# Turning k, q and u of the last two batches by transposing DMA, and a ring of three in the planned order of row loads

## The chip, the core and the metric

The kernel runs on one core of a Trainium2 chip. The metric is the device time of one execution in microseconds, as the median of several runs. One further execution was recorded by the hardware profiler; every duration of a single instruction below is from that execution.

## What is computed

Four batches, eight heads, 768 tokens, head size 64. A retention recurrence gives y, which is laid side by side over the heads as x of 768 tokens by 512 channels; a mixer follows, first over the tokens, then over the channels:

```python
for t in range(S):
    state = gamma * state + einsum('bhd,bhe->bhde', k[:, :, t], v[:, :, t])
    y[:, :, t] = scale * einsum('bhd,bhde->bhe', q[:, :, t], state)
x = y.transpose(0, 2, 1, 3).reshape(B, S, H * D)
h = relu(x.T @ w_tok1) @ w_tok2          # over the 768 tokens, 256 hidden
u = x + h.T
out = u + relu(u @ w_ch1) @ w_ch2        # over the 512 channels, 1536 hidden
```

## The kernel before

The recurrence is done in blocks of 128 tokens. For each batch b there are four **fronts** (b, p), one for each pair of heads (p, 128 channels together), and one **back**.

A front loads the f32 rows of k, q and v of two heads (`kf`, `qf`, `vf`, 384 KB each, L227 to L245), and casts them to f16 tiles `k16` (VectorE, L257), `q16` and `v16` (GpSimd, L264), each of 128 tokens by six blocks by 128 channels. `turn` (L271 to L288) then makes the transposed tiles `kT` and `qT`, channels on partitions: six transposes of 128x128 on TensorE into a PSUM tile `fa` (L277), and one copy out of PSUM (L286), on ScalarE but for the first batch's kT. The state products (L299), the masked products within a block (L338, which read kT and qT), y (L359 and L362), the two token matmuls (L413 and L433) and the addition of the result to x (VectorE, L440) follow. The sum, u, is cast to f16 by GpSimd in two halves (tile `u16`, L447), turned by six more transposes (L457) and copied to `uT` (ScalarE, L466).

A back takes uT of all four fronts of its batch. Twice (once for each half of the tokens) it runs 48 matmuls against `wc1` (L497) with a Relu behind every four (L510), and then three groups of twelve matmuls against `wc2` (L526), each followed by the addition of x (L535) and a store of 256 KB (L542).

The order of all this is not that of the code: `arrange` is a list scheduler with estimated durations. It gives out the next operation by start time and priority; a front's work on TensorE goes ahead of a back's, so a back fills the time in which a front waits. What it gives out is then emitted, and each engine runs its own rows strictly in that order. For the row loads and stores the queue is SP's: a DMA at the head that waits for data holds every DMA behind it. A load is told apart only by an estimated transfer time, `dma`, which is added to a single clock called `free["DMA"]`; nothing limits in the plan how many DMAs SP has given out and not yet moved.

Two more details. In the first two batches q is loaded with longer runs (L232), which interleaves its tokens, and the copy to qT undoes that. And 54 matmuls of a zero tile (L184) fill TensorE in the first batch while it waits for data.

Of the kernel before, what the change touches and what calls it, by code (L numbers as in the profile page):

```python
# [11 lines left out]
F16 = mybir.dt.float16  # L12
# [5 lines left out]
def kernel(  # L18
# [11 lines left out]
    nc = tc.nc  # L30
    B, H, S, D = q.shape
    P = 128
    NC = S // P
    HC = NC // 2
    NP = H // 2
# [10 lines left out]
    sb = ctx.enter_context(tc.tile_pool(name="sb", bufs=1))  # L46
# [31 lines left out]
    for p in range(NP):  # L78
# [5 lines left out]
        out=mask, in_=mask, compare_op=ALU.is_ge, fill=0.0,  # L84
# [4 lines left out]
    for t in r16:  # L89
# [6 lines left out]
    wc2 = const_p.tile([P, NF, C], F16, name="wc2")  # L96


    BUFS = dict(kf=4, qf=4, vf=4, k16=3, q16=3, v16=4, kT=4, qT=4, U=3, am=8, x16=2, h1=4, u16=3,
                x=3, uT=3, h2=2, o=3, r16=NR, fa=5, ba=3)  # L100
    SEM, GUARD = 80, 100
    EARLY, LATE, DIRECT = 1000, 12, 3
    ops = []

    class Slot:
# [15 lines left out]
    def arrange():  # L121


        way = {}
        for op in reversed(ops):
            if op.first is not None:
                way[op] = way.get(op, 0) + op.lat + SEM
                for d in op.deps:
                    way[d] = max(way.get(d, 0), way[op])
        for op in ops:  # L130
            if op.first is not None:
                op.prio = (op.prio[0], 0, EARLY * op.first - way[op], op.first)
        free = dict(PE=5000, ACT=5000, DVE=4600, POOL=4000, SP=1300, DMA=1300)
        taken = {t: [] for t in BUFS}
        todo, order = list(ops), []
        while todo:
            best = []
            for op in todo:
                if any(d.end is None for d in op.deps):
                    continue  # L140
                start = free[op.eng]
                for d in op.deps:
                    if d.eng == op.eng and (d.dma or d.eng == "PE"):
                        continue
                    start = max(start, d.end + (30 if d.eng == op.eng else SEM) + op.guard)
                more = {}
                for s in op.takes:
                    q = taken[s.tag]
                    n = len(q) + more.get(s.tag, 0) - BUFS[s.tag]
                    more[s.tag] = more.get(s.tag, 0) + 1  # L150
                    if n >= 0:
                        old = q[n]
                        if any(u.end is None for u in old.users):
                            break
                        start = max([start] + [u.end + SEM for u in old.users])
                else:
                    best.append((start, op))
            t = min(b[0] for b in best)

            eng = min(best, key=lambda b: (b[0], b[1].prio))[1].eng  # L160
            start, op = min((b for b in best if b[1].eng == eng and b[0] <= t + 20),
                            key=lambda b: b[1].prio)
            free[op.eng] = start + op.occ
            op.start = start
            if op.dma:
                free["DMA"] = max(free["DMA"], start + 50) + op.dma
                op.end = free["DMA"] + 1600
            else:
                op.end = start + op.lat
            for s in op.takes:  # L170
                taken[s.tag].append(s)
            todo.remove(op)
            order.append(op)
        return order
# [3 lines left out]
    def tile_of(slot, pool, shape, dtype, tag=None):  # L178
        tag = tag or slot.tag
        slot.tile = pool.tile(shape, dtype, name=tag, bufs=BUFS[tag])  # L180
        if pool is ps:

            for _ in range(idle[0]):
                nc.tensor.matmul(slot.tile, zero[:, :P], zero, start=True, stop=True)  # L184
            idle[0] = 0
        return slot.tile
# [11 lines left out]
    x_add, uT_done, y_done, t1_done, t2_done = {}, {}, {}, {}, {}  # L198
# [3 lines left out]
    def front(b, p):  # L202
        first = b == 0
# [3 lines left out]
        def op(eng, occ, lat, emit, deps=(), takes=(), uses=()):  # L207
            n[0] += 1
            pr = (0 if eng == "PE" else 1, b, n[0] + LATE * p, p)
            o = Op(eng, pr, occ, lat, emit, deps, takes, uses, guard=g if eng == "PE" else 0)  # L210
            o.first = p if first else None
            return o
# [3 lines left out]
        X, UT = xs[b], uTs[b]  # L216
        pc = slice(p * P, (p + 1) * P)

        def half(hf):
            return slice(hf * HC, (hf + 1) * HC)  # L220


        sl, ld = {}, {}
        for nm, src in (("k", k), ("q", q), ("v", v)):
            sl[nm] = Slot(nm + "f")

            def emit(nm=nm, src=src):  # L227
                t = tile_of(sl[nm], sb, [P, 2 * NC, D], FP)
                rows = src[b, 2 * p:2 * p + 2]
                if nm == "q" and b < 2:  # L230

                    dma = nc.sync.dma_start(  # L232
                        out=t.rearrange("p (h f i) d -> p h f (i d)", h=2, f=2),
                        in_=rows.rearrange("h (f p i) d -> p h f (i d)", f=2, p=P))
                else:
                    dma = nc.sync.dma_start(out=t, in_=rows.rearrange("h (c p) d -> p (h c) d", p=P))  # L236
                if b == 1:
                    tc.add_manual_dep(
                        dma.ins, wops["c1", 1].ins.ins.name,
                        mybir.DependencyInfo(mybir.DependencyClass.Sync, mybir.DependencyReason.DATA),  # L240
                        reason="the weights come first")
            ld[nm] = Op("SP", (0, b, p), 100, 100, emit,
                        deps=[load_done[-1]] + ([wops["c1", 1]] if b == 1 else []),
                        takes=[sl[nm]], dma=1200 if nm == "q" and b < 2 else 1750)
            load_done.append(ld[nm])  # L245

        K, Q, V = Slot("k16"), Slot("q16"), Slot("v16")
# [23 lines left out]
        def turn(src, dst, dep, eng):  # L271
            T = Slot("fa")

            def emit():
                T.tile = tp = tile_of(T, ps, [P, 512], FP).bitcast(F16)
                for c in range(NC):
                    nc.tensor.transpose(tp[:, c * P:(c + 1) * P],  # L277
                                        src.tile[:, c].rearrange("p h d -> p (h d)"), ident16)
            t = op("PE", 340, 500, emit, [dep, t1_done.get(b * NP - 1) if b > 1 else None], [T], [src])

            def emit():
                d, o = tile_of(dst, sb, [P, S], F16), T.tile[:, :S]
                if dst is QT and b < 2:
                    d = d.rearrange("d (f p i) -> d f i p", f=2, i=HC)
                    o = o.rearrange("d (f i p) -> d f i p", f=2, i=HC)
                (nc.scalar.copy if eng == "ACT" else nc.vector.tensor_copy)(d, o)  # L286
            occ = dict(ACT=1350 if dst is QT and b < 2 else 700, DVE=470)[eng]
            return op(eng, occ, occ + 90, emit, [t], [dst], [T])  # L288
        kt = turn(K, KT, kc, "DVE" if first else "ACT")
        qt = turn(Q, QT, qc, "ACT")  # L290


        ST, US, RS = Slot("fa"), Slot("U"), Slot("r16")
# [126 lines left out]
            h1 = tile_of(H1, sb, [P, NJ, P], F16)  # L420
            nc.scalar.activation(h1.rearrange("p j c -> p (j c)"), T1.tile[:, :NJ * P], AF.Relu)
        hr = op("ACT", 300, 380, emit, [t1], [H1], [T1])
        tt = []
        T = Slot(FA)
        for hf in range(2):
            T2, U16 = Slot(FA), Slot("u16")

            def emit(hf=hf, T2=T2):
                acc = tile_of(T2, ps, [P, 512], FP)
# [13 lines left out]
            x_add[b, p, hf] = ad  # L443

            def emit(hf=hf, U16=U16):
                u = tile_of(U16, sb, [P, HC, P], F16)
                nc.gpsimd.tensor_copy(u, X.tile[:, half(hf), pc])  # L447
            uc = op("POOL", 450, 510, emit, [ad], [U16], [X])
            if first:
                T = Slot(FA)  # L450

# [9 lines left out]
            if first or hf == 1:  # L461
                def emit(hf=hf, T=T):
                    if UT.tile is None:
                        tile_of(UT, sb, [P, NP, S], F16)
                    t = slice(hf * SH if first else 0, (hf + 1) * SH)
                    nc.scalar.copy(UT.tile[:, p, t], T.tile[:, t])  # L466
                tk = [UT] if (b, "uT") not in uT_done else []
                dep = [] if tk else [uT_done[b, "uT"]]
                e = op("ACT", 380 if first else 700, 480 if first else 800, emit, [tt[-1]] + dep, tk,
                       [T] if tk else [T, UT])  # L470
                if tk:
                    uT_done[b, "uT"] = e
                for s in range(2):
                    if not first or s == hf:
                        uT_done[b, p, s] = e
        return kc, qc, vc


# [123 lines left out]
```

## Time and profile before

| | |
|---|---|
| median of three runs | 217.54 us (216.63 to 217.7) |
| the profiled execution | 216.79 us, of which the span of its instructions is 215.1 us |
| VectorE, ScalarE, GpSimd busy | 113.2, 113.3 and 61.4 us |
| DMA | 29.42 MB, of it 25.17 MB on the hardware queue that SP feeds |
| granted TensorE clock | 0.999 |

The times of runs are of the whole execution; the profile's times count from the span's start, and the 1.7 us between span and execution lie around it. TensorE's matmuls are pipelined: the duration of a row of matmuls holds the fill and drain, so the cost of a group is better read from the start of the next row. What the engines wait for is shown with the prediction.

### The profile page before, as it was taken

How to read it: one execution, taken by the hardware profiler on the slowest of the kernel's cores; microseconds unless marked ns; L12 is line 12 of the kernel's file. 1: busy time of each engine (PE TensorE's matmuls, PEld its weight loads, DVE VectorE, ACT ScalarE, POOL GpSimd, SP SyncE). 2: the span in 40 equal slices, each digit the busy share in tenths (PEclk: the TensorE clock that was granted, in tenths of full speed). 3: DMA queues.
4: the chain of work that ended last, by engine and by line, in shares of the span. 5: the costliest groups of instructions: out<-in, count | busy, mean ns of one | idle time of the engine just before them, and what ended most of it. 6: DMA issues, size and time to landing. Idle time of an engine off the chain costs nothing.

```text
span 215.1 us, 5027 instructions
## 1 busy us (share of the span) xinstructions
PE 206.7 (96%) x2042; PEld 129.6 (60%) x2042; DVE 113.2 (53%) x291; ACT 113.3 (53%) x229; POOL 61.4 (29%) x107
## 2 busy tenths in 40 slices
PE   6898898999999999999999999999999999999993
PEld 1564486664667677676667676667645645545552
DVE  6387895017998876886865886673112012012021
ACT  6246467772887537668536787344721712703700
POOL 2337943023345455453444113302100000000000
PEclk9999999999999999999999999999999999999999
DMA  6999999999999999999921100012002012012012
GB/s 171 245 242 233 191 203 208 222 216 265 222 235 237 253 240 217 217 223 259 217 105 49 52 2 3 0 67 83 0 10 111 28 46 103 0 49 98 0 52 98
DMA packets 73591, 29.42 MB, mean 137 GB/s; under 512 B 62688, under 2 KB 70112, under 8 KB 73568
## 3 DMA queue, kind: packets, MB, share of 16 engines
q1 hardware_dynamic: 69904, 25.17, 53.8%
q0 software_dynamic: 3664, 3.93, 11.2%
q8 instruction: 16, 0.26, 0.5%
q14 instruction: 7, 0.06, 0.1%
HBM read 26.74 MB, written 6.29 MB: 154 GB/s over the span
## 4 chain that ended last, share of the span: by engine, by line
PE 85%; SPq 5%; DMA 4%; ACT 2%; DVE 1%; issue 1%; POOL 0%; DVEq 0%
PE ba L497 30%; PE ba L526 29%; PE fa L277 4%; PE fa L433 4%; PE fa L413 4%; DMA kf<-in_k_dram 4%; PE fa L338 3%; SPq L236 3%; PE fa L362 3%; SPq L232 2%; PE fa L457 2%; PE fa L359 2%; PE fa L299 2%; PE ba L413 1%; PE ba L184 1%; ACT qT L286 1%
## 5 line engine op out<-in xcount | busy, mean ns | idle before, releaser
L526 PE MATMUL ba<-wc,h 128*128 128x512 f16 (+1 forms) x300 | 68.1, 371 | 0.0
L497 PE MATMUL ba<-uT,wc 128*128 128x384 f16 x384 | 68.1, 326 | 0.0
L510 ACT ACTIVATE h<-ba 128x384 f16<-128x384 f32 x96 | 46.6, 491 | 40.0 <-PE ba L497 39.5
L497 PEld LDWEIGHTS <-wc 128*128 128x128 f16 x384 | 35.9, 98 | 22.5
L535 DVE TENSOR_TENSOR o<-x,ba 128x512 f32<-128x512 f32 (+1 forms) x25 | 16.6, 664 | 59.2 <-PE ba L526 59.0
L526 PEld LDWEIGHTS <-h 128*128 128x128 f16 x300 | 27.7, 98 | 26.2
L345 DVE TENSOR_TENSOR am<-fa,mask 128x384 f16<-128x384 f32 x64 | 33.0, 550 | 7.8 <-PE fa L338 7.5
L264 POOL CAST q<-qf 128x768 f16<-128x768 f32 x16 | 13.4, 840 | 32.4 <-DMA qf<-in_q_dram 23.2
L390 POOL CAST x<-x 128x384 f16<-128x384 f32 x30 | 15.1, 512 | 23.8 <-ACT x L373 14.8
L286 ACT COPY qT<-fa 128x768 f16<-128x768 f16 x16 | 18.1, 1129 | 6.8 <-PE fa L277 6.8
L447 POOL CAST u<-x 128x384 f16<-128x384 f32 x32 | 15.9, 507 | 19.4 <-DVE x L440 17.5
L257 DVE TENSOR_SCALAR k<-kf,gk 128x384 f16<-128x384 f32 x32 | 13.8, 472 | 9.0 <-DMA kf<-in_k_dram 9.0
L184 PE MATMUL fa<-zero 128*128 128x512 f16 x54 | 15.8, 424 | 2.4 <-DVE zero L52 1.3
L311 DVE SCALAR_TENSOR_TENSOR U<-U,gp,fa 128x64 f32<-128x64 f32 x64 | 17.6, 275 | 1.0
L373 ACT ACTIVATE x<-fa,gy 128x192 f32<-128x192 f32 (+1 forms) x42 | 15.1, 419 | 5.0 <-PE fa L362 4.5
L264 POOL CAST v<-vf 128x768 f16<-128x768 f32 x16 | 13.2, 828 | 12.1 <-PE fa L362 7.3
L466 ACT COPY uT<-fa 128x768 f16<-128x768 f16 x12 | 9.5, 794 | 13.2 <-PE fa L457 13.2
L318 ACT ACTIVATE r<-U 64x320 f16<-64x320 f32 x16 | 7.5, 466 | 13.6 <-DVE U L311 13.4
L440 DVE TENSOR_TENSOR x<-x,fa 128x384 f32<-128x384 f32 x24 | 12.6, 548 | 3.7 <-PE fa L433 3.6
L362 PE MATMUL fa<-v,am 128*128 128x64 f16 x192 | 14.1, 193 | 0.0
L413 PEld LDWEIGHTS <-wt 128*128 128x128 f16 x192 | 11.8, 98 | 2.6 <-issue 0.4
L433 PEld LDWEIGHTS <-wt 128*128 128x128 f16 x192 | 11.6, 98 | 2.0
(52 smaller groups left out, 195.0 us busy)
## 6 DMA issues: line engine op xcount, KB each, us to landing
kf<-in_k_dram SPq DMA_DIRECT2D x16, 384.0 KB, 6.5
qf<-in_q_dram SPq DMA_DIRECT2D x16, 384.0 KB, 6.3
vf<-in_v_dram SPq DMA_DIRECT2D x16, 384.0 KB, 6.1
out_dram<-o SPq DMA_DIRECT2D x23, 256.0 KB, 2.0
wc<-in_moe_w_ch_dram POOLq DMA_DIRECT2D x1, 1536.0 KB, 19.1
wc<-in_moe_w_ch_dram POOLq DMA_DIRECT2D x1, 1024.0 KB, 11.8
wt<-in_moe_w_tok_dram POOLq DMA_DIRECT2D x2, 384.0 KB, 7.0
wc<-in_moe_w_ch_dram POOLq DMA_DIRECT2D x1, 512.0 KB, 6.9
```

Source lines behind the costliest of these rows:

```text
L184: nc.tensor.matmul(slot.tile, zero[:, :P], zero, start=True, stop=True)
L264: nc.gpsimd.tensor_copy(t.rearrange("p c h d -> p h c d"), src.tile.rearrange("p (h c) d -> p h c d", h=2))
L286: (nc.scalar.copy if eng == "ACT" else nc.vector.tensor_copy)(d, o)
L311: nc.vector.scalar_tensor_tensor(U[:, c], U[:, c - 1], gp[:, p:p + 1], o, ALU.mult, ALU.add)
L345: nc.vector.tensor_tensor(am, src[:, :HC], mask, ALU.mult)
L362: nc.tensor.matmul(o[:, j * D:(j + 1) * D], AM[2 * hf + j].tile[:, i], V.tile[:, c, j], start=(c == 0), stop=(c == 0 or j == 1))
L413: nc.tensor.matmul(acc[:, jt * P:(jt + 1) * P], wt1[:, i, jt * P:(jt + 1) * P], X16.tile[:, i], start=(i == 0), stop=(i == NC - 1))
L433: nc.tensor.matmul(acc[:, i * P:(i + 1) * P], wt2[:, jt, t], H1.tile[:, jt], start=(jt == 0), stop=(jt == NJ - 1))
L497: nc.tensor.matmul(acc[:, :SH], w[:, ct, f * P:(f + 1) * P], UT.tile[:, ct, sh * SH:(sh + 1) * SH], start=(ct == 0), stop=(ct == NP - 1))
L510: nc.scalar.activation(H2.tile[:, ft], A.tile[:, :SH], AF.Relu)
L526: nc.tensor.matmul(A.tile[:, :CW], H2.tile[:, ft, i * P:(i + 1) * P], wc2[:, ft, cs], start=(ft == 0), stop=(ft == NF - 1))
L535: nc.vector.tensor_tensor(o[:, :CW], X.tile[:, sh * HC + i, cs], A.tile[:, :CW], ALU.add)
```

## The change

Three things are changed, all in `arrange` and `front`.

1. For the batches from the third on (`XK = XQ = XU = 2`), `turn` is replaced for k and q by `crossbar`: one transposing DMA on SP's queue, from `k16` or `q16` straight to `kT` or `qT` (192 KB each, both in SBUF). No PSUM tile, no TensorE work and no ScalarE copy is left of it. The gate that held the turns of the later batches until the last first token matmul of the batch before (`t1_done`) is not among the crossbar's conditions.
2. For the same batches u is cast by GpSimd into one tile `u16w` for both halves (two buffers), and one transposing DMA on SP's queue makes that front's part of `uT`. 24 transposing DMAs are added in all: eight each for k, q and u.
3. The planner gets a list `ring` of the planned ends of SP's transfers. A DMA on SP isn't planned to start before the third last one given out has been moved (`RING = 3`). This moves loads and stores against each other in SP's queue from the second batch on.

`LONG = 2` only gives the old condition `b < 2` a name.

```diff
-    BUFS = dict(... u16=3,
+    BUFS = dict(... u16=3, u16w=2,
+    LONG, XK, XQ, XU, XBAR, RING = 2, 2, 2, 2, 1500, 3
...
-        todo, order = list(ops), []
+        todo, order, ring = list(ops), [], []
...
                 start = free[op.eng]
+                if op.dma and op.eng == "SP" and len(ring) >= RING:
+                    start = max(start, ring[-RING])
...
                 op.end = free["DMA"] + 1600
+                if op.eng == "SP":
+                    ring.append(free["DMA"])
...
-        kt = turn(K, KT, kc, "DVE" if first else "ACT")
-        qt = turn(Q, QT, qc, "ACT")
+
+        def crossbar(src, dst, dep):
+            def emit():
+                d = tile_of(dst, sb, [P, S], F16)
+                return nc.sync.dma_start_transpose(
+                    out=d.rearrange("d (c t) -> d c t", t=P),
+                    in_=src.tile.rearrange("p c h d -> p (c h d)"))
+            return Op("SP", (-1, b, p), 100, 100, emit, [dep], [dst], [src], dma=XBAR)
+        kt = crossbar(K, KT, kc) if b >= XK else turn(K, KT, kc, "DVE" if first else "ACT")
+        qt = crossbar(Q, QT, qc) if b >= XQ else turn(Q, QT, qc, "ACT")
...
-        tt = []
-        T = Slot(FA)
+        tt, uc = [], None
+        wide = b >= XU
+        T, UW = Slot(FA), Slot("u16w")
...
-            T2, U16 = Slot(FA), Slot("u16")
+            T2, U16 = Slot(FA), UW if wide else Slot("u16")
...
-                u = tile_of(U16, sb, [P, HC, P], F16)
+                if wide:
+                    u = tile_of(U16, sb, [P, NC, P], F16) if hf == 0 else U16.tile
+                    u = u[:, half(hf)]
+                else:
+                    u = tile_of(U16, sb, [P, HC, P], F16)
                 nc.gpsimd.tensor_copy(u, X.tile[:, half(hf), pc])
-            uc = op("POOL", 450, 510, emit, [ad], [U16], [X])
+            new = hf == 0 or not wide
+            uc = op("POOL", 450, 510, emit, [ad, uc] if wide else [ad], [U16] if new else [], [X] if new else [X, U16])
+            if wide:
+                continue
...
+        if wide:
+            def emit():
+                if UT.tile is None:
+                    tile_of(UT, sb, [P, NP, S], F16)
+                return nc.sync.dma_start_transpose(
+                    out=UT.tile[:, p].rearrange("d (c t) -> d c t", t=P),
+                    in_=UW.tile.rearrange("p c d -> p (c d)"))
+            tk = [UT] if (b, "uT") not in uT_done else []
+            e = Op("SP", (-1, b, p), 100, 100, emit, [uc] + ([] if tk else [uT_done[b, "uT"]]), tk,
+                   [UW] if tk else [UW, UT], dma=XBAR)
+            if tk:
+                uT_done[b, "uT"] = e
+            for s in range(2):
+                uT_done[b, p, s] = e
```

What this does to the engines' own orders is seen at three places. The first is SP's queue at the start of the third batch. Before, the loads of its first two fronts (k, q, v) stand there with one store of the first back between them:

```order
L236 DMA kf<-in_k_dram 128x12x64
L236 DMA qf<-in_q_dram 128x12x64
L236 DMA vf<-in_v_dram 128x12x64
L542 DMA out_dram<-o 128x512
L236 DMA kf<-in_k_dram 128x12x64
L236 DMA qf<-in_q_dram 128x12x64
L236 DMA vf<-in_v_dram 128x12x64
```

Now the same queue, from the same load on (the code's lines have moved: L236 is L241, the transposing DMAs of k and q are L298):

```order
L241 DMA kf<-in_k_dram 128x12x64
L241 DMA qf<-in_q_dram 128x12x64
L241 DMA vf<-in_v_dram 128x12x64
L241 DMA kf<-in_k_dram 128x12x64
L241 DMA qf<-in_q_dram 128x12x64
L298 DMA_TRANSPOSE kT<-k_1285 128x6x128
L298 DMA_TRANSPOSE qT<-q_1330 128x6x128
L241 DMA vf<-in_v_dram 128x12x64
L298 DMA_TRANSPOSE kT<-k_1407 128x6x128
L298 DMA_TRANSPOSE qT<-q_1447 128x6x128
L241 DMA kf<-in_k_dram 128x12x64
```

Three stores of the first back now stand ahead of these rows, among the loads of the second batch, where before the first store of all stood behind the first three of them; and four transposing DMAs, which wait for the casts of k and q, stand ahead of the third front's k.

The second place is SP's queue around the last loads, those of front (3, 3). Before, they are followed by stores alone, twenty of the 25:

```order
L236 DMA kf<-in_k_dram 128x12x64
L236 DMA qf<-in_q_dram 128x12x64
L236 DMA vf<-in_v_dram 128x12x64
L542 DMA out_dram<-o 128x512 x18
L542 DMA out_dram<-o 128x256 x2
```

Now (L577 is the store, L501 the transposing DMA of u):

```order
L298 DMA_TRANSPOSE qT<-q_2398 128x6x128
L501 DMA_TRANSPOSE uT<-u16w 128x6x128
L298 DMA_TRANSPOSE kT<-k_2438 128x6x128
L298 DMA_TRANSPOSE qT<-q_2455 128x6x128
L577 DMA out_dram<-o 128x512 x3
L241 DMA kf<-in_k_dram 128x12x64
L241 DMA qf<-in_q_dram 128x12x64
L241 DMA vf<-in_v_dram 128x12x64
L298 DMA_TRANSPOSE kT<-k_2691 128x6x128
L298 DMA_TRANSPOSE qT<-q_2723 128x6x128
L501 DMA_TRANSPOSE uT<-u16w 128x6x128 x2
L577 DMA out_dram<-o 128x512 x3
```

The last three loads now stand behind twelve stores instead of five, that is, behind the whole of the first two backs, and behind 19 transposing DMAs.

The third place is TensorE where front (2, 0) begins. Before, its state products (L299) follow the turn of its q:

```order
L277 MATMUL fa<-ident_96,q_1286 128x128
L277 LDWEIGHTS q_1286
L277 MATMUL fa<-ident_96,q_1286 128x128
L299 LDWEIGHTS k_1234
L299 MATMUL fa<-v_1330,k_1234 64x64
```

Now they (L312) follow the turn of u of the second batch (L478), and no turn of k or q of this front stands anywhere on the engine:

```order
L478 MATMUL fa<-ident_96,u_1573 128x128
L478 LDWEIGHTS u_1573
L478 MATMUL fa<-ident_96,u_1573 128x128
L312 LDWEIGHTS k_1285
L312 MATMUL fa<-v_1377,k_1285 64x64
```

Over the whole engine 144 matmuls and their 144 weight loads are gone, 48 each for k, q and u; no other matmul is added or lost, but fronts and backs of the last two batches are woven differently. On ScalarE 24 copies are gone; VectorE and GpSimd keep all their instructions in another order.

More of the change, by code (lines that the diff above doesn't have):

```diff
@@ L96 @@
     wc2 = const_p.tile([P, NF, C], F16, name="wc2")
-    BUFS = dict(kf=4, qf=4, vf=4, k16=3, q16=3, v16=4, kT=4, qT=4, U=3, am=8, x16=2, h1=4, u16=3,
+    BUFS = dict(kf=4, qf=4, vf=4, k16=3, q16=3, v16=4, kT=4, qT=4, U=3, am=8, x16=2, h1=4, u16=3, u16w=2,
                 x=3, uT=3, h2=2, o=3, r16=NR, fa=5, ba=3)
@@ L229, in emit @@
                 rows = src[b, 2 * p:2 * p + 2]
-                if nm == "q" and b < 2:
+                if nm == "q" and b < LONG:
                     dma = nc.sync.dma_start(
@@ L243, in front @@
                         deps=[load_done[-1]] + ([wops["c1", 1]] if b == 1 else []),
-                        takes=[sl[nm]], dma=1200 if nm == "q" and b < 2 else 1750)
+                        takes=[sl[nm]], dma=1200 if nm == "q" and b < LONG else 1750)
             load_done.append(ld[nm])
@@ L282, in emit @@
                 d, o = tile_of(dst, sb, [P, S], F16), T.tile[:, :S]
-                if dst is QT and b < 2:
+                if dst is QT and b < LONG:
                     d = d.rearrange("d (f p i) -> d f i p", f=2, i=HC)
@@ L286, in emit @@
                 (nc.scalar.copy if eng == "ACT" else nc.vector.tensor_copy)(d, o)
-            occ = dict(ACT=1350 if dst is QT and b < 2 else 700, DVE=470)[eng]
+            occ = dict(ACT=1350 if dst is QT and b < LONG else 700, DVE=470)[eng]
             return op(eng, occ, occ + 90, emit, [t], [dst], [T])
-        kt = turn(K, KT, kc, "DVE" if first else "ACT")
-        qt = turn(Q, QT, qc, "ACT")
+        def crossbar(src, dst, dep):
[7 more added lines that the diff above has]
+        qt = crossbar(Q, QT, qc) if b >= XQ else turn(Q, QT, qc, "ACT")
         ST, US, RS = Slot("fa"), Slot("U"), Slot("r16")
```

## The prediction

> **What bounds the kernel now.** I read the page first: busy times, the slices, the chain.
>
> ```profile
> PE 206.7 (96%) x2042; PEld 129.6 (60%) x2042; DVE 113.2 (53%) x291; ACT 113.3 (53%) x229; POOL 61.4 (29%) x107
> ...
> PE   6898898999999999999999999999999999999993
> ...
> PEclk9999999999999999999999999999999999999999
> DMA  6999999999999999999921100012002012012012
> ...
> PE 85%; SPq 5%; DMA 4%; ACT 2%; DVE 1%; issue 1%; POOL 0%; DVEq 0%
> ```
>
> TensorE is busy in 96% of the span, full in every slice after the first seven or eight, at full clock, and is 85% of the chain. The DMA row is the second thing to see: full to slice 20 (some 108 us), nearly empty behind it. So the kernel is bound by TensorE's work, and next to it, in the first half, stands a full DMA queue. The timeline of TensorE shows whether "busy" is also dense:
>
> ```profile
> 100.15 0.50 PE L457 MATMUL fa<-ident,u 128*128 128x128 f16 x6
> 100.48 0.22 PE L359 MATMUL fa<-r,qT 128*128 128x128 f16 x1
> ...
> 100.82 0.50 PE L277 MATMUL fa<-ident,k 128*128 128x128 f16 x6
> 101.16 0.50 PE L277 MATMUL fa<-ident,q 128*128 128x128 f16 x6
> 101.59 0.35 PE L299 MATMUL fa<-v,k 128*64 128x64 f16 x10
> 101.87 0.34 PE L338 MATMUL fa<-qT,kT 64*128 64x128 f16 x6
> ...
> 102.80 0.83 PE L413 MATMUL fa<-x,wt 128*128 128x128 f16 x12
> 103.47 0.22 PE L362 MATMUL fa<-v,am 128*128 128x64 f16 x2
> ```
>
> The columns are start, duration, engine, line. Each group starts while the one before it drains. A turn of six costs from its start to the next start 0.33 us (100.15 to 100.48) or 0.34 us (100.82 to 101.16), not its 0.50. In the same way a group of six L338 costs 0.27, ten L299 0.28, twelve L413 or L433 0.67 us, half a front's y (100.48 to 100.82) 0.34.
>
> ```profile
> 164.62 7.96 PE L497 MATMUL ba<-uT,wc 128*128 128x384 f16 x48
> 172.42 7.93 PE L526 MATMUL ba<-wc,h 128*128 128x512 f16 x36
> 180.19 7.96 PE L497 MATMUL ba<-uT,wc 128*128 128x384 f16 x48
> ...
> 203.56 7.96 PE L526 MATMUL ba<-wc,h 128*128 128x512 f16 x48
> ```
>
> The end is pure back work: 7.80 us for 48 of L497 (0.1625 each), 7.77 for 36 of L526 (0.216 each). TensorE ends at 203.56 + 7.96 = 211.5.
>
> **What is removed.** These are the groups by line:
>
> ```profile
> L277 PE MATMUL fa<-ident,k 128*128 128x128 f16 x96 | 8.3, 225 | 1.1 <-DVE k L257 1.1
> L277 PE MATMUL fa<-ident,q 128*128 128x128 f16 x96 | 8.0, 219 | 0.2 <-POOL q L264 0.2
> ...
> L457 PE MATMUL fa<-ident,u 128*128 128x128 f16 x72 | 7.0, 219 | 0.0
> ```
>
> Half of k's and q's 96 go (two of four batches), and 48 of the 72 u turns in `fa`. That is 24 groups of six, at 0.34 us: **8.2 us** of TensorE, all of it on the path, since the engine is dense there. If nothing is late, the profiled execution goes from 216.8 to 208.6.
>
> ScalarE loses the copies, off the path:
>
> ```profile
> L286 ACT COPY qT<-fa 128x768 f16<-128x768 f16 x16 | 18.1, 1129 | 6.8 <-PE fa L277 6.8
> L286 ACT COPY kT<-fa 128x768 f16<-128x768 f16 x12 | 9.6, 803 | 1.9 <-PE fa L277 1.9
> L466 ACT COPY uT<-fa 128x768 f16<-128x768 f16 x12 | 9.5, 794 | 13.2 <-PE fa L457 13.2
> ```
>
> 24 copies of about 0.8 us are some 19 us of an engine that is 53% busy. They lie beside TensorE's work, so I count them at nothing; at most they spare a rare wait.
>
> **What is added: work on SP's queue and the DMA engines.** Here is that queue before:
>
> ```profile
> 57.64 1.34 SPq L236 DMA_DIRECT2D kf<-in_k_dram  x1
> ...
> 79.68 1.70 SPq L236 DMA_DIRECT2D vf<-in_v_dram  x1
> 81.48 1.70 SPq L236 DMA_DIRECT2D kf<-in_k_dram  x1
> ...
> 94.17 2.66 SPq L542 DMA_DIRECT2D out_dram<-o  x1
> ...
> 104.55 107.79 SPq L542 DMA_DIRECT2D out_dram<-o  x20
> ```
>
> The second column is how long SP sat in the issue; at 1.7 us it is held by the transfers ahead of it, so SP's rhythm is the transfers'. Eight loads go out from 79.68 to 94.17: 1.81 us each. From 57.64 (k of the third batch) to 104.55 there are 24 loads and five stores in 46.9 us, so a store costs (46.9 - 24 x 1.81) / 5 = 0.7 us. After the last byte a completion takes up to 2 us, as a store alone shows, where a load queued behind others takes 6.5:
>
> ```profile
> kf<-in_k_dram SPq DMA_DIRECT2D x16, 384.0 KB, 6.5
> ...
> out_dram<-o SPq DMA_DIRECT2D x23, 256.0 KB, 2.0
> ```
>
> The trace shows no transposing DMA; call its price **X**. Below: its 192 KB at a store's rate, 0.7 x 192/256 = 0.5 us. Above: it moves 768 pieces of 256 bytes, but if it breaks them up while turning, say eightfold into 32-byte pieces (an assumption), those are 6144, and at a load's time per piece (1.81 us / 1536 = 1.18 ns) 7.2 us. The nearest row is the load with its pieces of 256 bytes: 768 x 1.18 ns = 0.9 us. I take 0.9 to 1.7 us.
>
> What X may cost follows from TensorE's clock. In the new order, behind the point at which the products of front (3, 3) (L351) need its kT and qT, there stand 144 matmuls of L532, 120 of L561 with 512 columns and 24 with 256, and 2.7 us of that front: 23.4 + 25.9 + 2.6 + 2.7 = 54.6 us. TensorE without waits ends at 211.5 - 8.2 = 203.3, so these tiles are due at 148.7. SP reaches the third batch at 57.64 plus three stores that now stand ahead, 59.7. Up to qT of (3, 3) it then has 24 loads (43.4 us), nine stores (6.3 us) and 21 crossbar transfers, and 2 us to land: 51.7 + 21 X, in 89.0 us. So **X may be 1.78 us; each 0.1 us above costs 2.1 us, and at 2.17 us the 8.2 us are spent.** Crossbar transfers of the last fronts' u stand behind this point; uT of (3, 3) is covered by the second half of the third back.
>
> The same budget from a later point, since SP may have idled: uT of (2, 3) can't go before its u is there. In the new order this is 35.0 us of TensorE ahead of 148.7 (96 of L532, 48 of L561 and three fronts' worth). From the second token matmul to u in f16 the trace has
>
> ```profile
> 149.67 0.83 PE L433 MATMUL fa<-h,wt 128*128 128x128 f16 x12
> ```
>
> ```profile
> 150.90 0.97 POOL L447 CAST u<-x 128x384 f16<-128x384 f32 x2 [3.22 <-DVE x L440]
> ```
>
> so 2.2 us from its start to the end of the casts. Then eight loads, four stores, seven crossbars and the landing: 2.2 + 14.5 + 2.8 + 2 + 7 X, and X may be 1.9. At X = 0.9 this leaves 7 us of slack, at 1.7 it leaves 1.6.
>
> The three stores moved ahead go where their data is ready, and free the output tiles earlier; their 2.1 us come off the same budget. The dropped gate costs nothing.
>
> New waits are likely at places where a product now follows a landing. A late front has left one mark on TensorE before:
>
> ```profile
> 80.00:90.00 10.00, 9.55 (x132) 6.94 (x130) 6.82 (x19) 6.04 (x9) 4.70 (x9) 1.00 1.22 215
> ```
>
> PE has 9.55 of 10 us there, 0.45 us lost where the third batch joins. I allow three such (its kT, its uT, the fourth batch's kT): 1.4 us. **Sum: 216.8 - 8.2 + 1.4 = 210.0** for the profiled execution; the median of the runs stands 0.75 us above it, so 210.7.
>
> On X two pages of the Trainium skill disagree. "VectorE: DVE Perf Modes", section "The three transpose paths", gives 1309 ns for one 128x128 crossbar transpose against 390 ns on TensorE, and its rules for kernel authors prefer TensorE where PSUM will do. No run here shows the former; TensorE's 56 ns here (0.34/6) are far under its figure, which so isn't a price in a dense stream. "DMA: Bandwidth & Descriptors", section "Latency and other measured facts", has 261 GB/s for a transposing DMA; as an estimate, 0.75 us for 192 KB, and the sum above would stand.
>
> **Rivals.**
>
> *The queue's order gives part of it back.* X is small, but SP takes its rows in order, and a crossbar transfer or store that waits holds loads behind it. For: there are 24 more such points, and the slack above is 2 to 7 us. Against: that slack, and DMA was able to run ahead before. With 3 to 6 us lost the execution takes 211.6 to 214.6, the median 212 to 215.5.
>
> *The crossbar is dearer than 2.17 us* (slower). The place is SP's queue from the third batch to front (3, 3); TensorE waits at L351. For: the upper bound, and that DMA is already full there. Against: the nearest row. The middle of the bounds by ratio, with the row as the lower, sqrt(0.9 x 7.2) = 2.5 us, gives 208.6 + 21 x (2.5 - 1.78) = 223.7, the median 224; 3 us give 235.
>
> *Broken-up pieces at full price*, X = 7.2: 208.6 + 21 x 5.4 = 322, the median 323. For it speaks only the bound. The page with 1309 ns would, for six blocks one after another, come to 7.9 us, an estimate from its figure.
>
> *TensorE doesn't take the 8.2 us*, because what is left is paced by PSUM tiles or by Relu on ScalarE and the gaps close elsewhere: 216 to 218. Against it speaks the dense start-to-start rhythm of all groups.
>
> **How the numbers follow.** Forecast (X up to 1.78, waits of 0 to 3 us) 0.52; queue order 0.14; dearer crossbar 0.22; full price 0.07; not taken 0.05. About 0.5% (1.1 us) is what a measurement here can tell from no change. Faster: 0.52, 0.09 of the second and 0.01 of the third case, 0.62. Same: 0.05 of the second, 0.01 of the third, 0.04 of the last, 0.10. Slower: 0.28. The range: below, no new wait and half of the old ones gone too, 208; above, it leaves out the full price and the half of the third case beyond X = 2.75 us, 229 + 0.75, 230. The forecast's own range is 208 to 213.
>
> **What would show it.** Right: no row of L282 after the second batch; TensorE 144 matmuls fewer and busy to about 199 us; the rhythm on SP between two queued crossbar issues under 1.7 us; DMA full until some 140 us, L351 of (3, 3) starting near 149. Wrong: idle of TensorE ahead of L351 or L532 in the last two batches, released by the crossbar's DMA (X too dear) or with SP waiting on VectorE or GpSimd just before (order); a rhythm over 2.2 us settles for slower.

## The result, and the profile after

The changed kernel takes **208.82 us** (median of four runs, 208.47 to 209.11) against 217.49 for the kernel before: a ratio of 0.961, with a 95% interval of 0.958 to 0.964. The profiled execution went from 216.79 to 208.47 us, its span from 215.1 to 206.8.

The page of the changed kernel, as shown of before (busy times, slices, chain):

```profile
PE 198.9 (96%) x1898; PEld 120.5 (58%) x1898; DVE 114.8 (56%) x291; ACT 96.2 (47%) x205; POOL 61.9 (30%) x107
...
PE   6899899999999999999999999999999999999993
...
DMA  6999999999999999989995899996722012012012
...
PE 83%; SPq 5%; DMA 4%; DVE 3%; ACT 2%; issue 1%; POOL 0%; DVEq 0%
```

TensorE has 144 matmuls less and is 7.8 us less busy (206.7 to 198.9), yet as dense as before: 96% in both. ScalarE is 17 us less busy, which shows nowhere in the time. The DMA row, before full to slice 20 and then empty, is now busy to slice 29 (some 150 us), if less in slices 22 and 28: what was nearly empty up to there is now filled.

TensorE's timeline near the end (start, duration, engine, line; L351 are the products of front (3, 3)):

```profile
148.72 0.51 PE L351 MATMUL fa<-qT,kT 64*128 64x128 f16 x12
...
195.26 7.96 PE L561 MATMUL ba<-wc,h 128*128 128x512 f16 x48
```

The prediction counted 148.7 for the start of the first and 203.3 for the end of the second; they came at 148.72 and 203.22 (195.26 + 7.96). Ahead of this stands, on SP's queue:

```profile
136.17 2.21 SPq L241 DMA_DIRECT2D vf<-in_v_dram  x1
143.43 1.22 SPq L298 DMA_TRANSPOSE kT<-k  x1
144.76 1.22 SPq L298 DMA_TRANSPOSE qT<-q  x1
146.07 2.58 SPq L501 DMA_TRANSPOSE uT<-u16w  x2
```

SP had given out nothing for five microseconds ahead of the last four, so they show a crossbar's own rhythm: 1.22 us in the issue, 1.33 us from start to start (143.43 to 144.76). From issue to landing (median, the last number of each line) it takes, in the view of DMA issues, a few microseconds:

```profile
kT<-k SPq DMA_TRANSPOSE x8, 3.5
qT<-q SPq DMA_TRANSPOSE x8, 2.8
uT<-u16w SPq DMA_TRANSPOSE x8, 3.8
```

The qT of front (3, 3), given out at 144.76, landed 2.8 us later, at 147.6: 1.2 us before L351 used it. That is all the room that was left at this point.

And the packets, a line of the page in the kernel before and in the changed one:

```profile
DMA packets 73591, 29.42 MB, mean 137 GB/s; under 512 B 62688, under 2 KB 70112, under 8 KB 73568
```

```profile
DMA packets 92790, 34.13 MB, mean 165 GB/s; under 512 B 81888, under 2 KB 89312, under 8 KB 92768
```

The 24 transfers brought 19,199 packets, 800 each, for 4.71 MB, 196 KB each: 245 bytes a packet on average.

### The profile page after: what moved, and what is told of

The parts are those of the page before. It is cut to its first block, busy times and chain, and to the rows that moved or that the text cites. A ratio compares the mean times of both kernels' runs of the same rounds, so it can differ in the third digit from the quotient of the medians.

```text
span 206.8 us, 4738 instructions
## 1 busy us (share of the span) xinstructions
PE 198.9 (96%) x1898; PEld 120.5 (58%) x1898; DVE 114.8 (56%) x291; ACT 96.2 (47%) x205; POOL 61.9 (30%) x107
## 4 chain that ended last, share of the span: by engine, by line
PE 83%; SPq 5%; DMA 4%; DVE 3%; ACT 2%; issue 1%; POOL 0%; DVEq 0%
PE ba L532 31%; PE ba L561 29%; PE fa L426 4%; DMA kf<-in_k_dram 4%; PE fa L447 4%; PE fa L351 3%; SPq L241 3%; PE fa L375 3%; SPq L237 2%; PE fa L372 2%; PE fa L282 2%; PE fa L312 2%; DVE k L262 1%; PE ba L426 1%; PE ba L189 1%
## 5 line engine op out<-in xcount | busy, mean ns | idle before, releaser
L262 DVE TENSOR_SCALAR k<-kf,gk 128x384 f16<-128x384 f32 x32 | 14.5, 495 | 7.6 <-DMA kf<-in_k_dram 7.5
L324 DVE SCALAR_TENSOR_TENSOR U<-U,gp,fa 128x64 f32<-128x64 f32 x64 | 17.1, 275 | 1.0
L291 ACT COPY qT<-fa 128x768 f16<-128x768 f16 x8 | 11.6, 1455 | 6.5 <-PE fa L282 6.5
L375 PE MATMUL fa<-v,am 128*128 128x64 f16 x192 | 13.9, 193 | 0.0
L375 PEld LDWEIGHTS <-am 128*128 128x128 f16 x192 | 12.1, 98 | 1.9
L465 POOL CAST u16w<-x 128x384 f16<-128x384 f32 x16 | 7.9, 506 | 14.7 <-DVE x L454 14.6
```

Source lines behind the costliest of these rows:

```text
L262: nc.vector.tensor_scalar(k16[:, :, j, :], src, gk[:, h:h + 1], None, ALU.mult)
L324: nc.vector.scalar_tensor_tensor(U[:, c], U[:, c - 1], gp[:, p:p + 1], o, ALU.mult, ALU.add)
L375: nc.tensor.matmul(o[:, j * D:(j + 1) * D], AM[2 * hf + j].tile[:, i], V.tile[:, c, j], start=(c == 0), stop=(c == 0 or j == 1))
```

## The experiments

Twelve kernels ran, in three groups; each group had its own runs of the kernel before (216.7, 216.9 and 217.1 us median), so the comparisons below go by the ratio to these. A difference of ratios times 217.5 is given as microseconds against the change (ratio 0.961).

The theory, A: the gain is the TensorE time of the 24 turns, and the crossbar hides in slack of SP's queue. The rivals are other parts of the change (ring, earlier stores, relief of ScalarE), and a queue without slack.

### Turns put back on TensorE

```diff
+        def idle_turn(src, dep):
+            T = Slot("fa")
+            def emit():
+                T.tile = tp = tile_of(T, ps, [P, 512], FP).bitcast(F16)
+                for c in range(NC):
+                    nc.tensor.transpose(tp[:, c * P:(c + 1) * P], ..., ident16)
+            op("PE", 340, 500, emit, [dep], [T], [src])
+        if b >= XK:
+            idle_turn(K, kc)
+            idle_turn(Q, qc)
+            idle_turn(K, kc)
```

> The changed kernel, with 24 groups of six transposes put back on TensorE (three in each front of the last two batches, of k, q and k) into PSUM tiles that nothing copies or reads; the crossbar still makes kT, qT and uT. Theory A (TensorE time is the whole gain): 24 x 0.34 = 8.2 us come back, 216 to 218 us. Rival F (relief of ScalarE, whose 24 copies stay away, is part of the gain): 211 to 215 us.

Measured 216.87 us against 216.88 for the kernel before: ratio 1.000 (0.999 to 1.001). The page:

```profile
PE 207.1 (96%) x2042; PEld 128.6 (60%) x2042; DVE 114.3 (53%) x291; ACT 96.3 (45%) x205; POOL 61.9 (29%) x107
```

ScalarE stays as light as in the change (96.3), TensorE is back at 207.1, and the time is that of before. The whole gain goes with the turns on TensorE; the relief of ScalarE gives none of it, nor does the dropped gate, which is still dropped here. The turns put back take PSUM tiles too, so this run alone doesn't tell the matmuls from their tiles. But before, TensorE stood idle only 0.45 us in all between 40 us and its last matmul, so waits for tiles can't have been worth more than that.

### The ring alone

```diff
-    LONG, XK, XQ, XU, XBAR, RING = 2, 2, 2, 2, 1500, 3
+    LONG, XK, XQ, XU, XBAR, RING = 2, 4, 4, 4, 1500, 3
```

> The ring of three in the planned order alone: k, q and u of all batches are turned on TensorE again, only the order of loads and stores differs from the kernel before. Theory A (the gain is the TensorE time of the 24 turns that are gone): no change against the kernel before, 216.5 to 218.0 us, ratio 0.995 to 1.002. Rival B (a good part of the gain is the earlier stores and better paced loads): 211 to 215 us.

217.33 us, ratio 1.003 (1.002 to 1.005). No gain; it is 0.3% slower, which the theory had not said. Rival B falls.

### k and q alone

```diff
-    LONG, XK, XQ, XU, XBAR, RING = 2, 2, 2, 2, 1500, 3
+    LONG, XK, XQ, XU, XBAR, RING = 2, 2, 2, 4, 1500, 3
```

> Crossbar for k and q alone, u turned on TensorE as before; ring kept. Theory A: 8 of the 24 groups of six come back, 8 x 0.34 = 2.7 us over the changed kernel, 211 to 212 us. Rival D (the copies of uT on ScalarE and the two u halves waiting for one another cost more than the turns): more than 4 us over it, 213 us and above.

211.28 us, ratio 0.975 (0.973 to 0.977), so 3.1 us over the change for eight groups of six, expected 2.7. The turns of u give their share, as those of k and q do.

### The crossbar without the ring

```diff
-    LONG, XK, XQ, XU, XBAR, RING = 2, 2, 2, 2, 1500, 3
+    LONG, XK, XQ, XU, XBAR, RING = 2, 2, 2, 2, 1500, 1000000
```

> The crossbar for k, q and u of the last two batches as in the change, but without the ring: SP's order is planned as in the kernel before, with any number of transfers given out ahead. Theory A with slack in SP's queue (X about 1.3 us, 1.78 allowed): the same as the change, 208 to 210 us. Rival C (the ring is what keeps the crossbar transfers from waiting behind loads; TensorE then waits at L351): 212 to 220 us.

214.64 us, ratio 0.992 (0.989 to 0.994): 6.7 us over the change, where 208 to 210 us were expected. The time is rival C's. So the ring, worth nothing by itself, carries most of the gain here. Four views show how: the first crossbar's row of SP's queue, without the ring and in the change; a window (PE's busy time is its second column, the granted clock and the DMA share stand near the end); pieces of the chain of waits (start, duration, what); and the busy times of its page:

```profile
81.36 2.54 SPq L298 DMA_TRANSPOSE kT<-k  x1
```

```profile
68.47 2.20 SPq L298 DMA_TRANSPOSE kT<-k  x1
```

```profile
130.00:140.00 10.00, 8.05 (x101) 5.56 (x99) 9.64 (x29) 2.56 (x7) 3.00 (x6) 0.83 0.69 169
```

```profile
133.82 0.47 DVE am L358
134.47 0.48 DVE am L358
134.97 0.48 DVE r L335
135.49 0.56 DVE am L358
```

```profile
PE 201.2 (94%) x1898; PEld 123.2 (58%) x1898; DVE 111.3 (52%) x291; ACT 96.8 (45%) x205; POOL 61.4 (29%) x107
```

The first crossbar goes out at 81.36, behind all twelve loads of the third batch; in the change it goes at 68.47, behind five. The fronts of the last two batches then come late and close together, and in the window above TensorE waits inside them: the chain there is a front's own, over VectorE, and from 133.8 to 136 no matmul of a back stands in it. TensorE's timeline has no matmul of a back at all between the end of one back near 131.8 and the next one's first near 142: nothing is left to fill with. VectorE is busy 9.64 of the 10 us, which fits fronts that came together. The place is not the one that rival C named: behind 40 us TensorE's longest waits are for VectorE at L372 and L375, 1.2 and 1.0 us in all, and L351 isn't among them. TensorE lost 1.95 us in this window and ran at a granted clock of 0.83. That clock is a cost of its own: the same 1898 matmuls were busy 201.2 us here and 198.9 in the change, so some 2.3 of the 6.2 us between the two spans (213.0 and 206.8) are longer matmuls, and 3.9 are waits.

Rings of other depths:

> The change with a ring of four transfers ahead in the planned order in place of three. If the ring matters as a limit of any size (without it 5.8 us are lost): 208.5 to 210 us. If three is the depth at which the chip's queue holds SP, and one more is already planned too early: 210 to 213 us.

> The change with a ring of two in place of three. If being planned too late costs little, since SP then waits for casts anyway: 208.5 to 210 us. If the queue runs dry between transfers: 211 to 214 us.

208.14 us with four (ratio 0.959, 0.957 to 0.961) and 208.84 with two (0.962, 0.961 to 0.964). Neither can be told from three. What counts is that SP's order is planned with some limit.

### The price of a crossbar on the queue

Each crossbar is given out a second time into a spare tile:

```diff
+    spare = [const_p.tile([P, S], F16, name=f"spare_{i}") for i in range(4)]
+    again = [0]
+    def once_more(src):
+        t = spare[again[0] % 4]
+        again[0] += 1
+        nc.sync.dma_start_transpose(out=t.rearrange("d (c t) -> d c t", t=P), in_=src)
...
-                return nc.sync.dma_start_transpose(
+                ins = nc.sync.dma_start_transpose(
...
+                once_more(src.tile.rearrange("p c h d -> p (c h d)"))
+                return ins
```

> The changed kernel, with every crossbar transfer given out a second time into a spare tile that nothing reads; order otherwise as in the change. It doubles the price of a crossbar on SP's queue from about 1.3 to about 2.6 us. The budget in the prediction (21 transfers ahead of front (3, 3), free up to 1.78 us, 2.1 us lost for each 0.1 us above): 208.8 + 21 x (2.6 - 1.78) = 226 us, 220 to 232, with TensorE idle ahead of L351 in the last two batches. Rival E (the queue's slack is larger than that budget, since loads can move up wherever SP waits): 209 to 213 us.

229.98 us, ratio 1.060 (1.056 to 1.063): 21.5 us over the change, within the expected 220 to 232. The busy times of its page, two windows, and TensorE's longest waits:

```profile
PE 203.9 (89%) x1898; PEld 122.5 (54%) x1898; DVE 114.0 (50%) x291; ACT 96.3 (42%) x205; POOL 61.7 (27%) x107
```

```profile
100.00:110.00 10.00, 6.88 (x85) 4.60 (x86) 5.38 (x11) 3.15 (x8) 1.98 (x4) 1.00 1.05 174
...
140.00:150.00 10.00, 8.05 (x57) 3.50 (x57) 4.15 (x12) 0.47 (x1) 3.47 (x6) 0.83 1.33 192
```

```profile
PE fa L321 <- POOL v L276: 12.3, 4, 4.6
PE fa L360 <- DMA qT<-q: 3.1, 3, 2.0
```

TensorE waits at the state products for the cast of v (12.3 us), whose load stands behind crossbars in SP's queue, more than for the crossbar's own tiles (3.1). The expectation named the second place only. TensorE's matmuls, as many as in the change, are busy 5.0 us longer (203.9 against 198.9), at a granted clock of 0.83 in some of the windows; so some 5 of the 21.5 us are the clock and not the queue.

With the spare for k alone (`if src is K:` ahead of `once_more`, and none for u):

> The changed kernel with only the crossbar transfers of k given out twice, the second into a spare tile: 29 transfers at 1.33 us ahead of front (3, 3), 38.6 us of queue against 37.3 allowed. By the budget 1.3 us over, 209 to 212 us. Rival G (no threshold, each transfer on SP's queue costs TensorE in proportion: the 24 extra transfers cost 21.2 us, so 8 cost 7 us): 215 to 217 us.

214.22 us, ratio 0.989 (0.987 to 0.992), 6.2 us over the change and between the two expectations. The queue's own work grew by 8 x 1.33 = 10.6 us here and, with the extra transfers ahead of front (3, 3), by 21 x 1.33 = 27.9 above; the losses were 6.2 and, without the 5 us of the clock, some 16.5. So some 4 us were absorbed here (the mean granted clock was 0.997) and some 11 above. The budget had 89.0 - 51.7 - 21 x 1.33 = 9.4 us to absorb: about right for the sum of many transfers, too much for these eight, where it left a loss of 1.3 us and 6.2 came. The slack is not one number; it depends on where the extra transfers stand.

In the changed kernel, a row of the waits of SP's queue and two of VectorE's timeline show where part of it goes:

```profile
SPq L298 <- DVE k L262: 8.1, 3, 5.0
```

```profile
141.56 0.56 DVE L390 TENSOR_TENSOR x<-fa,gyw 128x384 f32<-128x384 f32 x1 [1.46 <-PE fa L375]
142.04 1.33 DVE L262 TENSOR_SCALAR k<-kf,gk 128x384 f16<-128x384 f32 x2
```

The k of (3, 3), given out at 134.62, landed 4.7 us later, at 139.3. But VectorE, which runs its rows in order, first waited for TensorE at L390 and cast k from 142.04 on. SP stood before kT until 143.43; the budget had SP busy with transfers all the way.

### More crossbar

From the second batch on, for k, q and u (`LONG, XK, XQ, XU = 1, 1, 1, 1`), for u alone (`XU = 1`), and for k alone (`XK = 1`):

> Crossbar for k, q and u from the second batch on, 36 transfers in place of 24; q's long runs only in the first batch. TensorE loses 12 more groups, 4.1 us, but 33 crossbar transfers, not 21, now stand ahead of the tiles of front (3, 3), so each may cost 37.3 / 33 = 1.13 us, and at the 1.33 us that they stand apart in the changed kernel 6.6 us are lost: 208.8 - 4.1 + 6.6 = 211 us, 209 to 215. Rival (slack in the queue is larger than the budget): 204.7 us.

> Crossbar for k and q from the third batch on as in the change, for u from the second: 28 transfers. Four groups less on TensorE, 1.4 us. Budget: 25 transfers ahead of front (3, 3), 37.3 / 25 = 1.49 us each against 1.33, so it holds: 207.4 us, 207 to 208. Rival (the tighter queue makes fronts late at other places): 209 to 212 us.

> Crossbar for k from the second batch on, q and u as in the change: 28 transfers, four groups (1.4 us) less on TensorE than the change. Theory A with room in the queue: 207.4 us. Rival H (the second batch's loads are still coming from 35 to 58 us; kT lands later than a turn would make it, and the first back runs out as filler, as the u of the second batch did): 210 to 216 us.

223.01 us (ratio 1.028, 1.025 to 1.032), 211.36 (0.974, 0.971 to 0.977) and 208.97 (0.964, 0.960 to 0.967): the first two lose 14.7 and 2.9 us against the change; the third can't be told from it, and so lacks the 1.4 us that were to be won. The budget said 211, 207.4 and 207.4. The kernel with u of the second batch points to the reason, in SP's queue, in TensorE's timeline, and in a window:

```profile
84.08 2.72 SPq L501 DMA_TRANSPOSE uT<-u16w  x1
```

```profile
84.61 0.51 PE L351 MATMUL fa<-qT,kT 64*128 64x128 f16 x12
...
88.60 0.35 PE L312 MATMUL fa<-v,k 128*64 128x64 f16 x10 [0.81 <-POOL v L269]
...
91.32 2.11 PE L532 MATMUL ba<-uT,wc 128*128 128x384 f16 x12
```

```profile
80.00:90.00 10.00, 7.83 (x110) 5.32 (x109) 9.03 (x23) 1.58 (x4) 2.77 (x5) 1.00 0.98 193
```

The first back ends near 84.6. The second can't start before the last uT of its batch, which is given out only at 84.08 and landed 4.6 us later, at 88.7; TensorE's order then has rows of the front ahead of the first use, at 91.32. In between TensorE has a front alone and loses 2.2 us of ten in the window. The profiled execution took 209.71 us at a granted clock of 1.0; the five others had 0.984 to 0.992, so the trace shows less of the loss than the median. In the last two batches a back still runs when uT is turned; in the second none does. With k alone, where u is still turned on TensorE, the same window has a gap too:

```profile
80.00:90.00 10.00, 8.30 (x109) 5.45 (x107) 8.06 (x23) 3.43 (x9) 3.66 (x6) 1.00 0.94 196
```

The 1.7 us lost there are more than the four groups are worth. So it is not the crossbar of u as such: in both kernels nothing is left to fill with between the first back and the second. That is read from the rows; no run tests it by itself.

In the kernel with all three the clock is a large part of the loss. The busy times of its page and two windows:

```profile
PE 202.9 (92%) x1826; PEld 122.0 (55%) x1826; DVE 116.1 (52%) x291; ACT 86.2 (39%) x193; POOL 63.1 (29%) x107
```

```profile
80.00:90.00 10.00, 3.61 (x53) 3.02 (x52) 5.54 (x15) 1.48 (x4) 3.73 (x7) 0.78 1.15 204
90.00:100.00 10.00, 7.00 (x76) 5.30 (x76) 7.00 (x18) 1.69 (x5) 4.68 (x9) 0.50 1.27 199
```

TensorE was busy 3.61 of ten microseconds in the first and had a granted clock of 0.50 in the second. With 12 groups less its matmuls should be busy 198.9 - 4.1 = 194.8 us and were 202.9: some 8 us are longer matmuls, and the rest is waits. This kernel also loads q of the second batch in the short runs, which was not tested apart.

### The planner's price

> The change with the planner's price of a crossbar at the 1.33 us that the trace shows, in place of 1.5. If the order is limited by how exact the prices are: 207.5 to 208.5 us. If a spare 0.17 us per transfer in the plan is what keeps TensorE from waiting: 209.5 to 212 us.

207.84 us, ratio 0.958 (0.957 to 0.960), the fastest of all kernels here, 0.6 us under the change. The intervals of the two ratios overlap, so a gain over the change is not shown.

## Why the prediction was right, and where it was not

- **TensorE is the bound and loses 24 x 0.34 = 8.2 us.** The profiled execution lost 8.3. Shown by the turns that were put back: the time of before returned.
- **Due times by the clock of TensorE** (148.7 and 203.3): met within 0.1 us, since nothing was late.
- **The 1.4 us for new waits was mis-sized.** The new order's only wait behind the first 40 us is 0.31 us, for VectorE; none is for a crossbar. These are the wait, and the window in which before 0.45 us were lost:

```profile
108.43 0.23 PE L372 MATMUL fa<-r,qT 128*128 128x128 f16 x1 [0.31 <-DVE r L335]
```

```profile
80.00:90.00 10.00, 10.00 (x112) 5.88 (x110) 9.02 (x26) 4.26 (x9) 4.80 (x9) 1.00 1.19 220
```

  The 0.45 us of before from which I took the allowance was also misread as a late front. Its row:

```profile
88.47 0.35 PE L299 MATMUL fa<-v,k 128*64 128x64 f16 x10 [0.45 <-ACT uT L466]
```

  TensorE there waited for ScalarE's copy of uT, and not for a landing. The term makes 1.4 of the 1.9 us between 210.7 and 208.8; 0.4 more is the distance from the profiled execution to the median, 0.75 us before and 0.35 now.
- **X between 0.9 and 1.7 us: measured 1.33**, of which the issue itself takes 1.22. The upper bound by broken-up pieces falls with the packets: 800 a transfer and not 6144. By the Trainium skill's "VectorE: DVE Perf Modes", section "The three transpose paths", one block takes 1309 ns, so six one after another would take 7.9 us, an estimate; the trace, with 1.33 us for all six, doesn't agree. By the Trainium skill's "DMA: Bandwidth & Descriptors", section "Latency and other measured facts", a transposing DMA has 261 GB/s, which would make 0.75 us, an estimate; the trace, with 196.6 KB in 1.33 us or 148 GB/s, doesn't agree.
- **The budget (X up to 1.78 free, then in proportion) is right as a sum and too generous at single points.** With every transfer doubled the loss was about what it says, the clock set apart (16.5 us against 27.9 - 9.4 = 18.5). Single points are tighter, because SP also waits for casts, and because a load behind a crossbar is late in its turn: at 1.33 us the budget left 9.4 us, the last qT landed 1.2 us before its use, and eight more transfers cost 6.2 us in place of 1.3. The prediction's second budget, from u of (2, 3) on, left 35.0 - 21.5 - 7 x 1.33 = 4.2 us at the same place and has no wait for the cast either. Neither was a guide to the second batch, where the filler is missing.
- **The ring.** The prediction counted only the three stores that it moves ahead. That without it 6.7 of 8.5 us (0.039 of 217.5) are lost was not foreseen; the rival in which the queue's order gives part back, at a median of 212 to 215.5, describes that kernel (214.64). The budget has no term for the order, and would have said the same 210.7 without the ring. That the change came with one is why the forecast held; to this extent it was luck.

## What to carry to other kernels

Where one engine is dense from start to start, as TensorE was here, work that is taken off it is worth its start-to-start time, and that time can be read from two rows of the timeline. The engine or queue that takes the work over needs slack at each point of use, not in total: look for what runs as filler while the moved work is on its way, and move it only where there is some. When a queue that runs in order gets many new waits, its planned order needs some limit on the transfers given out ahead (two, three and four did alike here), or loads planned too early delay what stands behind them. And a wait of TensorE can cost more than its length: where it waited long here, its clock was lower for a while afterwards.

## What the runs showed of the hardware

A transposing DMA of 128 x 768 f16 within SBUF holds SP for 1.22 us in the issue even when nothing is queued, where a plain load of twice the bytes is given out in 0.39, as this row of SP's queue has it:

```profile
58.29 0.39 SPq L241 DMA_DIRECT2D vf<-in_v_dram  x1
```

In a stretch of the doubled kernel where only crossbars and their doubles are given out, 1.27 to 1.39 us apart, the DMA engines are busy at 0.76, and at 1.37 in another, where loads run:

```profile
149.50:154.50 5.00, 4.79 (x52) 3.00 (x51) 4.15 (x12) 3.42 (x9) 0.00 (x0) 1.00 0.76 146
...
138.00:142.00 4.00, 0.06 (x3) 0.05 (x4) 0.00 (x0) 0.00 (x0) 2.56 (x4) 1.00 1.37 226
```

This suggests that SP's issue rather than the engines sets the crossbar's rate. It is not shown: giving them out from another queue was not tried.

TensorE's granted clock fell in the kernels in which it waited long: to 0.50 in the window from 90 to 100 us of the kernel with the crossbar from the second batch on, after a window in which it was busy 3.61 of ten microseconds.
